# Decode step with a mixer MLP: the last rows of w4 in six small loads behind wq

## The chip, the core and the metric

The kernel runs on one core of one Trainium2 chip. Its time is the device time of one execution in microseconds; shown is the median of several runs. A profile is taken of one execution, and the times inside it count from the start of its span.

The core has a matrix engine (TensorE, PE in the profile), a vector engine (DVE), a scalar engine (ACT), GpSimd (POOL) and a queue engine (SyncE, SP), which issues nearly all transfers here. Transfers run on 16 DMA engines. Each of them works through the pieces (packets) that it was given in the order in which the transfers were issued, and leaves a mark in the trace when its share of a transfer has landed.

## The reference

Two branches start from the layer-normed token xn (1 x 512). The first is an attention over the last 4096 places of the cache, 32 heads of 128. The second is a mixer MLP; with one token all its shifted parts are zero.

```
xn = layernorm(x)
q  = xn @ wq                                  # 512 x 4096
s  = softmax(q . k_window / sqrt(128)) . v_window, heads joined, @ wo
x1 = xn + shifted(gelu(layernorm(xn) @ w1)) @ w2   # the shifted part is 0
h2 = gelu(layernorm(x1) @ w3) @ w4            # w3: 512 x 1376, w4: 1376 x 512
out = x + s * silu(x1 + h2)
```

Weights and caches are bf16. The windows of keys and values are 32 MB each, wq and wo 4 MB each, w2, w3 and w4 3.3 MB together.

## The kernel before

Heads are worked on in eight groups of four (G = 4). A group's keys are one tile of 4 MB (128 partitions of 32 KB), and so are its values. In step s (the loop at the end of the kernel) group s gets its scores and group s - 2 its weighted values (LAG = 2). Scores are split between engines: DVE multiplies and reduces 64 to 80 of the 128 columns (`k_vector`, L329 and L331), and TensorE turns the rest (L345), ACT copies them (L347) and TensorE multiplies (L353). The softmax and the sums over values follow one and two steps behind.

Before the loop TensorE works through the MLP and then q, in the order of the program: the first layer's products with w3 into `a_ps` (L236), the gelu on ACT (L239 to L241), the sum `hr_ps` over w2 (L250) and w4 (L255), its spreading over partitions (L156), then the 128 products of `qT_ps` with wq (L271), and the spreading of q over partitions (L283), which the first product of DVE (L329) needs.

w4 has 1376 rows: 1024 in eight chunks of 128 (`w4_sb`), 32 in a ninth, and 320 extra rows in eight chunks of 40 (NE = 5, 8 x NE = 40). These last are `w4_few`, a tile of 64 partitions with eight rows of w4 (8 KB) on each partition that is used. L97 loads them in two transfers of 20 partitions, onto partitions 0 to 19 and 32 to 51, in an order of rows [...]. The other partitions are zeroed on POOL (L94), which the first of the two waits for. Since the rows then lie in another order than the gelu's results, a small matrix `few`, made from the identity on DVE (L184 to L186), reorders those in a matmul (L243), and a cast (L246) brings them back to bf16.

All large loads go through one function (L79) on the queue of SP, in the order of the program: w2, w3, w4, w4's ninth chunk, w4_few, wq, then the keys of group 0 in two halves, the keys of groups 1 and 2, then values and keys in turn, with wo between them. Transfers take eight semaphores in turn, so each waits for the landing of the one that had its semaphore before. Key tiles have three buffers and value tiles two, the latter in the memory that the weights leave (`wts`).

Of the kernel before, what the change touches and what calls it, by code (L numbers as in the profile page):

```python
# [8 lines left out]
P = 128  # L9
BF16 = mybir.dt.bfloat16  # L10
FP32 = mybir.dt.float32
# [10 lines left out]
NE = 5  # L22
# [7 lines left out]
def kernel(  # L30
# [14 lines left out]
    nc = tc.nc  # L45

    Bb, Sq, D = A_x.shape
# [18 lines left out]
    const = ctx.enter_context(tc.tile_pool(name="const", bufs=1))  # L66
    small = ctx.enter_context(tc.tile_pool(name="small", bufs=1))
    ps_misc = ctx.enter_context(tc.tile_pool(name="ps_misc", bufs=1, space=PSUM))
# [7 lines left out]
    wts = wts_guard.__enter__()  # L76

    def load(dst, src):
        return tc.keep_in_program_order(nc.sync.dma_start(out=dst, in_=src))  # L79
# [10 lines left out]
    w4_sb = wts.tile([P, 9, D], BF16, name="w4_sb")  # L90
    load(w4_sb[:, 0:8, :], B_w4[0:8 * P, :].rearrange("(p c) n -> p c n", p=P))
    load(w4_sb[0:32, 8, :], B_w4[F - 32:F, :])
    w4_few = wts.tile([64, 8, D], BF16, name="w4_few")
    nc.gpsimd.memset(w4_few[:], 0.0)  # L94
    for c in range(2):
        f0 = 8 * P + 32 * NE * c
        load(w4_few[32 * c:32 * c + 4 * NE],  # L97
             B_w4[f0:f0 + 32 * NE, :].rearrange("(b a t) n -> a b (t n)", b=4, a=NE))
    wq_sb = wts.tile([P, KC, HD], BF16, name="wq_sb")

    load(wq_sb[:].rearrange("p c n -> p (c n)"), A_wq.rearrange("(a b c) n -> b a (c n)", a=4, c=KC))

    def load_kv(pool, cache, g, cuts=(0, CP)):
        t = pool.tile([P, CP, Dh], BF16, tag="kv", name="kv")
        src = cache[0, G * g:G * g + G, W0:, :].rearrange("a (b c) d -> b a (c d)", b=PB)
        dst = t[:].rearrange("p c d -> p (c d)")
        for c0, c1 in zip(cuts, cuts[1:]):
            load(dst[:, c0 * Dh:c1 * Dh], src[:, :, c0 * Dh:c1 * Dh])
        return t

    ident_bf = const.tile([P, P], BF16, name="ident_bf")
# [68 lines left out]
        return xc, negmean, rstd  # L180


    few = const.tile([P, 2, 32], BF16, name="few")
    nc.vector.memset(few[:], 0.0)  # L184
    for c in range(2):
        nc.vector.tensor_copy(  # L186
            out=few[:, c, 0:4 * NE].rearrange("p (a b) -> p a b", b=4),
            in_=ident_bf[:, 4 * NE * c:4 * NE * (c + 1)].rearrange("p (b a) -> p a b", b=4))

    x_f = small.tile([P, KC], FP32, name="x_f")  # L190
    nc.vector.tensor_copy(out=x_f[:], in_=x_bf[:])
    xc, negmean, rstd = ln_stats(x_f[:], "x")
# [18 lines left out]
    for j in range(KC):  # L211
        for c in range(KC):
            nc.tensor.matmul(hs_ps[:, j:j + 1], lhsT=w2_sb[:, c, j::4],
                             rhs=shifted_bf[:, c:c + 1], start=(c == 0), stop=(c == KC - 1))
# [19 lines left out]
    for j, m in enumerate(chunks):  # L234
        for c in range(KC):
            nc.tensor.matmul(a_ps[0:m, j:j + 1], lhsT=w3_cols(c, j), rhs=z3_bf[:, c:c + 1],  # L236
                             start=(c == 0), stop=(c == KC - 1))
    a_bf = small.tile([P, 17], BF16, name="a_bf")
    nc.scalar.activation(out=a_bf[:, 0:8], in_=a_ps[:, 0:8], func=ACT.Gelu_apprx_tanh)  # L239
    nc.scalar.activation(out=a_bf[0:32, 8:9], in_=a_ps[0:32, 8:9], func=ACT.Gelu_apprx_tanh)  # L240
    nc.scalar.activation(out=a_bf[0:8 * NE, 9:17], in_=a_ps[0:8 * NE, 9:17], func=ACT.Gelu_apprx_tanh)  # L241
    af_ps = ps_misc.tile([64, 8], FP32, tag="misc", name="af_ps")
    nc.tensor.matmul(af_ps[:], lhsT=few[0:8 * NE].rearrange("p a b -> p (a b)"), rhs=a_bf[0:8 * NE, 9:17],  # L243
                     start=True, stop=True)
    af_bf = small.tile([64, 8], BF16, name="af_bf")
    nc.vector.tensor_copy(out=af_bf[:], in_=af_ps[:])  # L246

    hr_ps = ps_misc.tile([1, D], FP32, tag="misc", name="hr_ps")
    for c in range(KC):
        nc.tensor.matmul(hr_ps[:], lhsT=shifted_bf[:, c:c + 1], rhs=w2_sb[:, c, :], start=(c == 0),  # L250
                         stop=False)
    for i, m in enumerate(chunks):
        act = a_bf[0:m, i:i + 1] if i < 9 else af_bf[:, i - 9:i - 8]
        w = w4_sb[0:m, i, :] if i < 9 else w4_few[:, i - 9, :]
        nc.tensor.matmul(hr_ps[:], lhsT=act, rhs=w, start=False,  # L255
                         stop=(i == len(chunks) - 1))
    hr = wts.tile([1, D], FP32, name="hr")
    nc.vector.tensor_copy(out=hr[:], in_=hr_ps[:])  # L258
# [10 lines left out]
    for h in range(H):  # L269
        for c in range(KC):  # L270
            nc.tensor.matmul(qT_ps[:, h:h + 1], lhsT=wq_sb[:, c, h * Dh:(h + 1) * Dh],  # L271
                             rhs=xq_bf[:, c:c + 1], start=(c == 0), stop=(c == KC - 1))
# [7 lines left out]
    for i in range(0, H // G, 4):  # L280
        qb_ps = ps_tr.tile([P, 4, Dh], FP32, tag="pt", name="qb_ps")
        for k in range(4):
            nc.tensor.matmul(qb_ps[:, k, :], lhsT=sel[:, i + k, :, :].rearrange("k b a -> k (b a)"),  # L283
                             rhs=q_rows[:], start=True, stop=True)
# [355 lines left out]
```

## Time and profile before

| | |
|---|---|
| median of 8 runs | 195.96 us (194.87 to 196.84) |
| profiled execution | 195.74 us |
| its span | 193.9 us |
| busy: PE, DVE, ACT, POOL | 134.3, 145.6, 90.1, 5.9 us |
| moved by DMA | 79.08 MB, mean 408 GB/s |
| granted TensorE clock, mean | 0.708 |

The page gives busy times of each engine, the span in 40 slices, the transfers by queue, and the chain of work that ended last. Busy shares are averages over stages with different limits, so the prediction reads single instructions and what released them. A row of a view of instructions has its start and its length in us, the engine, the line, the operation, what it writes and reads, and in brackets how long the engine had been idle and what ended that. SP's rows are issues: how long the queue engine took to hand a transfer over, and not how long the transfer took.

### The profile page before, as it was taken

What the parts mean: (1) busy time and instruction counts of PE and PEld (TensorE: products, weight loads), DVE (VectorE), ACT (ScalarE), POOL (GpSimd) and SP (SyncE); (2) the same over time, 40 slices, a digit from 0 to 9 for tenths busy, and PEclk for the clock granted to TensorE, in tenths of its full rate; (3) what the DMA queues carried; (4) which work ended last, traced back from release to release, by engine and by line L of the source; (5) the groups of instructions that cost most, each with busy time, mean ns of one, the idle gap of its engine ahead of it and who ended that gap; (6) DMA issues with size and microseconds to landing.
All of it is one profiled execution on the core that took longest, in us unless ns stands there. A gap on an engine that the chain in (4) does not pass through costs nothing.

```text
span 193.9 us, 3919 instructions
## 1 busy us (share of the span) xinstructions
PE 134.3 (69%) x1696; PEld 96.1 (50%) x1696; DVE 145.6 (75%) x168; ACT 90.1 (46%) x197; POOL 5.9 (3%) x12
## 2 busy tenths in 40 slices
PE   0548978868646169159858882983696979886892
PEld 0447257657545144057438442941593358635281
DVE  1580013999999999998999999997999996952011
ACT  2002003887868165318856850681368156863100
POOL 8210000000000000000000000000000000000000
PEclk9999995797955555856797566558558885566675
DMA  5999999999999999999999999999999999999980
GB/s 197 416 442 433 426 429 436 427 429 433 433 431 433 433 429 433 433 433 433 429 433 429 433 433 395 466 433 433 429 426 427 422 433 389 466 405 372 399 304 0
DMA packets 4722, 79.08 MB, mean 408 GB/s; under 512 B 666, under 2 KB 1210, under 8 KB 1722
## 3 DMA queue, kind: packets, MB, share of 16 engines
q1 hardware_dynamic: 4554, 78.84, 95.7%
q8 instruction: 13, 0.21, 0.4%
q10 hardware_dynamic: 152, 0.00, 0.0%
q14 instruction: 3, 0.02, 0.0%
HBM read 78.84 MB, written 0.00 MB: 407 GB/s over the span
## 4 chain that ended last, share of the span: by engine, by line
DVE 51%; PE 27%; DMA 14%; issue 4%; ACT 2%; POOL 0%; POOLq 0%; ACTq 0%; SPq 0%
DVE S L331 29%; DVE prod L329 16%; DMA kv<-in_A_k_cache_dram 12%; PE oT L447 4%; PE pt L345 4%; PE ov L431 3%; PE hr_ps L255 3%; PE a_ps L236 2%; DMA x_bf<-in_A_x_dram 2%; PE oT L440 2%; PE qT_ps L271 2%; ACT kt L347 2%; PE y_ps L156 1%; PE sT L353 1%; PE hr_ps L250 1%
## 5 line engine op out<-in xcount | busy, mean ns | idle before, releaser
L331 DVE TENSOR_REDUCE S<-prod 128x20 f32<-128x2560 bf16 (+2 forms) x32 | 82.2, 2570 | 1.1
L347 ACT COPY kt<-pt 128x1024 bf16<-128x1024 bf16 (+1 forms) x56 | 54.6, 1007 | 17.4 <-PE pt L345 16.7
L345 PE MATMUL pt<-ident_bf,kv 128*128 128x128 bf16 x444 | 47.5, 278 | 3.9 <-DMA kv<-in_A_k_cache_dram 3.8
L329 DVE TENSOR_TENSOR prod<-kv,q_bc 128x2560 bf16<-128x2560 bf16 (+2 forms) x32 | 43.5, 1361 | 2.6 <-ACT q_bc L285 1.3
L345 PEld LDWEIGHTS <-kv 128*128 128x128 bf16 x444 | 38.7, 128 | 8.2 <-DMA kv<-in_A_k_cache_dram 4.8
L353 PE MATMUL sT<-qT_bf,kt 128*128 128x4 bf16 x444 | 20.7, 168 | 15.0 <-ACT kt L347 14.1
L353 PEld LDWEIGHTS <-kt 128*128 128x128 bf16 x444 | 17.2, 104 | 22.8 <-ACT kt L347 22.6
L431 PE MATMUL ov<-kv,pT 128*16 128x512 bf16 x224 | 23.2, 589 | 0.0
L447 PE MATMUL oT<-fold,ov_sb 128*128 128x4 f32 x56 | 10.8, 316 | 14.5 <-DVE rden L402 13.6
L447 PEld LDWEIGHTS oT<-fold,ov_sb 128*128 128x128 f32 x56 | 10.2, 273 | 15.6 <-DVE rden L402 14.0
L391 ACT ACTIVATE pT<-S,mb 128x128 bf16<-128x128 f32 x32 | 14.0, 584 | 0.3
L431 PEld LDWEIGHTS <-pT 128*16 128x16 bf16 x224 | 6.7, 123 | 14.6 <-issue 14.5
L461 ACT ACTIVATE o<-oT,rden 128x1 bf16<-128x1 f32 x20 | 3.6, 264 | 20.9 <-PE oT L447 20.9
L435 ACT COPY ov_sb<-ov 128x512 f32<-128x512 f32 x7 | 4.1, 585 | 16.4 <-PE ov L431 16.4
L362 ACT ACTIVATE own<-sT,par 128x48 f32<-128x48 f32 (+2 forms) x32 | 7.6, 358 | 3.6 <-PE sT L353 3.6
L457 DVE TENSOR_TENSOR o<-oT,rden 128x4 bf16<-128x4 f32 x3 | 0.5, 162 | 11.0 <-PE oT L447 8.5
L391 ACT ACTIVATION_READ_ACCUMULATOR pT<-S,mb 128x1 f32 x32 | 8.6, 267 | 0.0
L239 ACT ACTIVATE a_bf<-a_ps 128x8 bf16<-128x8 f32 x1 | 0.2, 177 | 14.4 <-PE a_ps L236 14.4
L384 PE MATMUL mb_ps<-md,par_t 5*128 5x4 f32 x16 | 4.2, 331 | 3.7 <-DVE md L379 3.7
L375 PE MATMUL mt_ps<-ident_f,m 128*1 128x128 f32 x8 | 2.8, 347 | 4.4 <-DVE rden L402 4.4
L236 PE MATMUL a_ps<-z_bf,w_sb 128*128 128x1 bf16 (+2 forms) x68 | 4.8, 204 | 1.5 <-DVE z_bf L219 1.5
L258 DVE COPY hr<-hr_ps 1x512 f32<-1x512 f32 x1 | 0.7, 678 | 6.8 <-PE hr_ps L255 6.8
(119 smaller groups left out, 101.6 us busy)
## 6 DMA issues: line engine op xcount, KB each, us to landing
kv<-in_A_k_cache_dram SPq DMA_DIRECT2D x7, 4096.0 KB, 31.7
kv<-in_A_v_cache_dram SPq DMA_DIRECT2D x7, 4096.0 KB, 29.9
wq_sb<-in_A_wq_dram SPq DMA_DIRECT2D x1, 4096.0 KB, 16.5
kv<-in_A_k_cache_dram SPq DMA_DIRECT2D x2, 2048.0 KB, 20.7
wo<-in_A_wo_dram SPq DMA_DIRECT2D x1, 2048.0 KB, 26.6
kv<-in_A_v_cache_dram SPq DMA_DIRECT2D x1, 2048.0 KB, 9.7
w_sb<-in_B_w_dram SPq DMA_DIRECT2D x1, 1376.0 KB
w_sb<-in_B_w_dram SPq DMA_DIRECT2D x1, 1024.0 KB, 9.0
```

What stands on the lines that cost most here:

```text
L236: nc.tensor.matmul(a_ps[0:m, j:j + 1], lhsT=w3_cols(c, j), rhs=z3_bf[:, c:c + 1], start=(c == 0), stop=(c == KC - 1))
L255: nc.tensor.matmul(hr_ps[:], lhsT=act, rhs=w, start=False, stop=(i == len(chunks) - 1))
L329: nc.vector.tensor_tensor(out=prod[:, 0:m, :], in0=kn[:, rows, :], in1=q_bc[:, g:g + 1, :].to_broadcast([P, m, Dh]), op=ALU.mult)
L331: nc.vector.tensor_reduce(out=st[g]["S"][:, rows], in_=prod[:, 0:m, :], axis=AX.X, op=ALU.add)
L345: nc.tensor.transpose(pt[:, c - c0, :], kn[:, c, :], ident_bf[:])
L347: nc.scalar.copy(out=kts[b][:, 0:c1 - c0, :], in_=pt[:, 0:c1 - c0, :])
L353: nc.tensor.matmul(st[g]["sT"][:, c - nd(g), :], lhsT=kt[:, c - c0, :], rhs=qT_bf[:, G * g:G * g + G], start=True, stop=True)
L362: nc.scalar.mul(s["own"][:, 0:m, a], s["sT"][:, 0:m, a], par[:, a:a + 1])
L384: nc.tensor.matmul(mb_ps[:], lhsT=par_t[:].rearrange("k b a -> k (b a)"), rhs=md[:], start=True, stop=True)
L391: nc.scalar.activation(out=s["pT"][:, :, a], in_=s["S"][:], func=ACT.Exp, scale=scale, bias=mb[:, a:a + 1], accum_out=s["sum"][:, a:a + 1])
L431: nc.tensor.matmul(s["ov"][r:r + 4 * G], lhsT=s["pT"][:, c:c + 4, :].rearrange("p i a -> p (i a)"), rhs=v[:, c:c + 4, :], start=False, sto ...
L447: nc.tensor.matmul(s["oT"][:], lhsT=s["ov_sb"][:, j, :], rhs=fold[:, G * j:G * j + G], start=(j == 0), stop=(j == 3))
```

## The change

The extra rows of w4 are loaded behind wq and in their plain order: partition p holds rows 1024 + 8 p to 1024 + 8 p + 7. The tile has 40 partitions, and six transfers of 25, 4, 4, 3, 2 and 2 partitions fill it. The first runs on five DMA engines with five packets each, each other one on as many engines as it has partitions[...]: 10, 10, 8, 7 and 5 packets on engines 0 to 4, where now each of them has 8. The memset of the tile, the matrix `few`, its matmul and the cast behind it go away, and the sum over w4 takes the gelu's results as they are.

```diff
-    w4_few = wts.tile([64, 8, D], BF16, name="w4_few")
-    nc.gpsimd.memset(w4_few[:], 0.0)
-    for c in range(2):
-        f0 = 8 * P + 32 * NE * c
-        load(w4_few[32 * c:32 * c + 4 * NE],
-             B_w4[f0:f0 + 32 * NE, :].rearrange("(b a t) n -> a b (t n)", b=4, a=NE))
+    w4_few = wts.tile([8 * NE, 8, D], BF16, name="w4_few")
     wq_sb = wts.tile([P, KC, HD], BF16, name="wq_sb")
 
     load(wq_sb[:].rearrange("p c n -> p (c n)"), A_wq.rearrange("(a b c) n -> b a (c n)", a=4, c=KC))
+    p0 = 0
+    for n in (25, 4, 4, 3, 2, 2):
+        load(w4_few[p0:p0 + n], B_w4[8 * (P + p0):8 * (P + p0 + n), :].rearrange("(p t) n -> p t n", t=8))
+        p0 += n
...
-    few = const.tile([P, 2, 32], BF16, name="few")
-    nc.vector.memset(few[:], 0.0)
-    for c in range(2):
-        nc.vector.tensor_copy(
-            out=few[:, c, 0:4 * NE].rearrange("p (a b) -> p a b", b=4),
-            in_=ident_bf[:, 4 * NE * c:4 * NE * (c + 1)].rearrange("p (b a) -> p a b", b=4))
...
-    af_ps = ps_misc.tile([64, 8], FP32, tag="misc", name="af_ps")
-    nc.tensor.matmul(af_ps[:], lhsT=few[0:8 * NE].rearrange("p a b -> p (a b)"), rhs=a_bf[0:8 * NE, 9:17],
-                     start=True, stop=True)
-    af_bf = small.tile([64, 8], BF16, name="af_bf")
-    nc.vector.tensor_copy(out=af_bf[:], in_=af_ps[:])
...
-        act = a_bf[0:m, i:i + 1] if i < 9 else af_bf[:, i - 9:i - 8]
         w = w4_sb[0:m, i, :] if i < 9 else w4_few[:, i - 9, :]
-        nc.tensor.matmul(hr_ps[:], lhsT=act, rhs=w, start=False,
+        nc.tensor.matmul(hr_ps[:], lhsT=a_bf[0:m, i:i + 1], rhs=w, start=False,
                          stop=(i == len(chunks) - 1))
```

## The prediction

> **What bounds the kernel now.** I read the page's slices and chain first, then the vector engine's instructions in order of time, then the issues of the sync queue, then TensorE's first 34 us, and last the landing marks that the trace keeps for every transfer: one for each DMA engine that took part.
>
> The page's transfer slices and its chain:
>
> ```profile
> DMA  5999999999999999999999999999999999999980
> ...
> DVE 51%; PE 27%; DMA 14%; issue 4%; ACT 2%; POOL 0%; POOLq 0%; ACTq 0%; SPq 0%
> ```
>
> The transfer engines are full from the first slice to the last but two, and yet the chain is mostly DVE. The two meet in one place, which the vector engine's instructions show:
>
> ```profile
> 133.97 0.29 DVE L369 TENSOR_REDUCE m<-S 128x1 f32<-128x128 f32 x1
> 135.24 1.49 DVE L329 TENSOR_TENSOR prod<-kv,q_bc 128x2560 bf16<-128x2560 bf16 x1 [0.99 <-DMA kv<-in_A_k_cache_dram]
> ```
>
> After the scores of group 5 DVE stands idle 0.99 us for the keys of group 6. The transfer's marks run from 131.86 (first engine) to 135.22 (last): DVE waits for the slowest of 16 engines, which is 3.36 us behind the fastest. Before this point DVE works nearly without a gap from 32.66 on, and each earlier key tile landed ahead of its use (k5: landed 110.91, used 115.60). After it comes a fixed row of compute to the end. So the time is what the slowest engine needs up to k6, plus about 60 us; a later start of DVE is free up to 0.99 us.
>
> Where the spread comes from: wq's marks are ten at 20.05 to 20.41, one at 21.89 and five at 22.45 to 22.65. The five are those that carried w4_few just ahead of wq, 8 packets of 8 KB each: 2.4 us, 0.31 us a packet (the packets are recorded at 309 to 356 ns, most near 310). This lag is still there 110 us later, since the rings are never empty. Two of the five are pushed back further, by 0.98 us before k1 lands and by 0.63 us before the first values land, beside packets of the instruction queue q14 at 35.4 and 57.3.
>
> The third view is the start, sync queue and TensorE:
>
> ```profile
> 4.41 1.73 SPq L79 DMA_DIRECT2D w_few<-in_B_w_dram  x2
> 6.18 0.60 SPq L79 DMA_DIRECT2D wq_sb<-in_A_wq_dram  x1
> 6.83 4.32 SPq L79 DMA_DIRECT2D kv<-in_A_k_cache_dram  x4
> ```
> ```profile
> 18.28 0.16 PE L243 MATMUL af_ps<-a_bf,few 40*64 40x8 bf16 x1 [0.37 <-ACT a_bf L241]
> 18.69 1.86 PE L250 MATMUL hr_ps<-w_sb,shifted_bf 128*1 128x512 bf16 x4 [0.25 <-DVE af_bf L246]
> 20.35 3.26 PE L255 MATMUL hr_ps<-w_sb,a_bf 128*1 128x512 bf16 x9
> 23.54 1.88 PE L255 MATMUL hr_ps<-w_few,af_bf 64*1 64x512 bf16 x8
> ...
> 27.14 3.41 PE L271 MATMUL qT_ps<-xq_bf,wq_sb 128*128 128x1 bf16 x128 [0.41 <-DVE bv L263]
> ```
>
> The reader should see that q (L271) stands behind the MLP's last sum (L255) on TensorE, and that w4_few, in place since 12.93, holds nobody up at 23.54.
>
> **The change part by part.** The sum is made against the profiled execution: 195.74 us, of which the span is 193.9 and 1.84 lie around it. The median is 195.96, 0.22 more.
>
> *Removed.* The memset of w4_few on POOL (3.51 us) held only w4_few's own issue; the rings still had w4 until 10.59. Two copies (0.24 us together) and a memset for `few` on DVE lie in its waits before 12 us. Nothing for both; without that cover 0.3 us on DVE, still inside the 0.99. The matmul at L243 and the cast behind it take 18.28 to 18.69 on the path to q: hr_ps starts 0.41 us earlier, and w4_few is wanted at 23.13.
>
> *Four more DMAs and their waits.* The eight lanes of completion semaphores shift. The later small loads now wait for x, w2, w3, w4 (the last at 10.59); k0's first half waits for w4's tail (10.82), its second half for wq (20.4 to 21.9), k1 and k2 for the first two w4_few loads. Queued behind each on SP are all later key loads. But k0's first half is on the rings by 12 and takes 4.9 us of every engine after wq (20.05 to 24.92 in the marks), and an issue reaches the engines in about 1.3 us (w2: 0.73 to 2.03). So second half and k1 (issued about 22 and 24) come in time: nothing. Without that cover each us of empty ring costs a us at k6.
>
> *Packets.* 25 rows on five engines are 5 each[...]. Engines 0 and 1 carry 2 packets more than now: 2 x 0.31 = +0.63 us. Engine 2 the same, engine 3 -0.31, engine 4 -0.94. If only packet counts mattered, k6 would be late by 0.63 if a pushed-back engine is 0 or 1.
>
> *Where the packets go.* [...] the rows at 310 ns next to wq's 32 KB at 1213 ns show no collision[...]
>
> By packet counts alone w4_few is complete at 20.1 + 3.13 = 23.2, TensorE waits 0.1 us, and k6 moves by +0.4 to +0.63. [...] Ends: nothing and +3.8. [...]
>
> *TensorE behind it.* With w4_few at 26.4 TensorE stands from 23.1 on; its last eight matmuls, h2, q (3.41), the broadcast and DVE's first product queue behind. Within L255 matmuls start 427 ns apart until 22.48 and 215 after. [...] Kept: 26.4 + 7 x 0.215 + 0.38 = 28.3 against 25.42 now, +2.9; dropped: 26.4 + 7 x 0.427 + 0.63 = 30.0, +4.6. Less the 0.99 of idle before k6: +1.9 or +3.6. Both run beside the transfers' +3.8 and don't add.
>
> *Sum.* The later of the two: +3.8[...]. k7 follows, as DVE needs 19.85 us from k6 to k7 and k7 landed at 155.06 for a use at 155.09; the last value tiles shift alike. 195.74 + 3.8 = 199.5, at the median 199.7.
>
> Also: what lies behind `few` and the copy of it moves by 128 to 160 bytes a partition, the value tiles among them. No row here times a tile at another offset; I take nothing.
>
> **Rivals.**
> *[...]packets count.* For it: no colliding row in the trace. TensorE hardly waits; k6 +0.4 to +0.63: 196.2 to 196.6, not slower by what can be told. [...]
> *Half of it.* [...] 197.4.
> *The right engines are spared.* If the two pushed-back engines are 2 and 3[...], the slowest becomes 0 or 1 at 3.1 instead of 3.36: -0.2, 195.7. More than 0.99 could not be gained here anyhow, as DVE's own work then sets k6.
> *The rings run dry* behind the new waits. Against it: the 4.9 us of cover. It would add to the first case, at most 2 us: 201.7.
>
> **How the numbers follow.** [...] 0.62 (with the dry rings' 0.04 in it); half 0.10; counts alone 0.20; spared 0.05; something faster that I don't see 0.03. Within 0.5% (0.98 us) is about what a measurement can't tell from no change. Slower: 0.62 + 0.10 + 0.02 of the third = 0.74; same 0.22; faster 0.04. The likeliest case alone has 198.7 to 200.6. The range 196.1 to 200.9 leaves out 0.14 below (the last two cases and a part of the third) and 0.05 above.
>
> **What would show it.** Right: packets of 8 KB of 0.6 to 1.6 us after wq; w4_few's last mark near 26.4; L255's eight matmuls starting there and L258 after 28; k6's marks spread over 6 to 7 us; DVE's wait before k6 of several us or a first product near 36. Wrong: those packets at 0.31, the last mark at 23.2, and k6 landing within 0.7 of 135.22; or a ring without packets between 20 and 30.

## The result

The changed kernel takes 197.79 us (median of 11 runs, 197.53 to 201.24) where the kernel before takes 195.11 us in the same comparison (median of 32 runs). The ratio is 1.0142, with a 95% interval from 1.0114 to 1.0170: slower by 1.4%. The profiled execution of the changed kernel took 197.55 us with a span of 195.7 us, against 195.74 and 193.9 before: +1.8 us in the two profiles, +2.7 us in the medians (the profiled execution before lies 0.63 above its median, the one after 0.24 below its own). The ratios here are of fast executions alone: one of the changed kernel's eleven (201.24 us) and the profiled one of own_counts6 further on (198.22 us) fell into a slower state and are left out of them.

The page's transfer slices and its chain, after:

```profile
DMA  6999999999999999999999999999999999999960
GB/s 206 447 418 420 296 425 455 420 435 425 429 439 417 442 429 419 442 442 429 425 429 435 432 429 402 452 435 429 439 429 429 420 429 390 467 415 400 394 243 4
...
DVE 48%; PE 22%; DMA 20%; ACT 4%; SPq 2%; issue 2%; ACTq 0%
```

The row of busy transfer engines looks as before: no gap in it. But the row below has one slice of 296 GB/s among slices of mostly 417 to 455, the fifth, from about 19.6 to 24.5 us. The engines are busy there and move a third less. The view by stretches shows it closer (columns: stretch, its length, busy time of PE, its weight loads, DVE, ACT and POOL, granted clock, busy share of the transfer engines, GB/s). Before:

```profile
20.00:22.00 2.00, 2.00 (x6) 0.57 (x5) 0.00 (x0) 0.00 (x0) 0.00 (x0) 1.00 0.88 369
22.00:24.00 2.00, 2.00 (x9) 0.57 (x8) 0.00 (x0) 0.00 (x0) 0.00 (x0) 1.00 1.06 451
24.00:26.00 2.00, 1.42 (x7) 0.47 (x6) 0.54 (x1) 0.00 (x0) 0.00 (x0) 1.00 1.00 426
```

After:

```profile
20.00:22.00 2.00, 2.00 (x6) 0.63 (x5) 0.00 (x0) 0.00 (x0) 0.00 (x0) 1.00 1.24 336
22.00:24.00 2.00, 1.49 (x4) 0.20 (x2) 0.00 (x0) 0.00 (x0) 0.00 (x0) 1.00 0.76 201
24.00:26.00 2.00, 0.60 (x3) 0.27 (x4) 0.00 (x0) 0.00 (x0) 0.00 (x0) 1.00 1.04 434
```

The packet records of that stretch (they carry a size and a time, but no engine) say what is slow. The 8 KB packets of w4_few mostly start at 309 to 325 ns and go up to 600 to 850 ns. The 16 KB packets of the first half of group 0's keys (k0), which other engines move at the same time and which otherwise take 611 to 620 ns, take 0.7 to 1.6 us between 20.9 and 23.6 us, all of them.

The landing marks carry this through. The six loads of w4_few left five, four, four, three, two and two of them, at 21.61 to 23.67, 22.44 to 23.15, 23.15 to 23.82, 24.25 to 24.36, 24.57 to 24.66 and 25.06 to 25.15; the two loads before left five each. A mark has a time but no number of its engine, so engine 0, engine 1 and so on are the author's names here and in what stands above. w4_few's last mark is at 25.15. k0's first half has its marks at 26.16 (first) to 29.97 (last), where before it had 24.92 to 27.53: the fastest engine is 1.24 us later and the slowest 2.44. Group 6's keys land at 133.07 to 137.50, before 131.86 to 135.22: 1.21 later on the fastest engine and 2.28 on the slowest.

The sync queue, TensorE's start and DVE, after:

```profile
2.63 0.64 SPq L79 DMA_DIRECT2D wq_sb<-in_A_wq_dram  x1
3.31 7.46 SPq L79 DMA_DIRECT2D w_few<-in_B_w_dram  x6
10.81 14.06 SPq L79 DMA_DIRECT2D kv<-in_A_k_cache_dram  x4
```
```profile
19.66 3.83 PE L241 MATMUL hr_ps<-w_sb,a_bf 128*1 128x512 bf16 x9
25.40 2.65 PE L241 MATMUL hr_ps<-w_few,a_bf 40*1 40x512 bf16 x8 [1.91 <-DMA w_few<-in_B_w_dram]
30.02 3.55 PE L257 MATMUL qT_ps<-xq_bf,wq_sb 128*128 128x1 bf16 x128 [0.41 <-DVE bv L249]
```
```profile
35.69 1.23 DVE L315 TENSOR_TENSOR prod<-kv,q_bc 128x2048 bf16<-128x2048 bf16 x1 [1.29 <-ACT q_bc L271]
...
137.56 1.48 DVE L315 TENSOR_TENSOR prod<-kv,q_bc 128x2560 bf16<-128x2560 bf16 x1
...
157.64 1.23 DVE L315 TENSOR_TENSOR prod<-kv,q_bc 128x2048 bf16<-128x2048 bf16 x1 [0.26 <-DMA kv<-in_A_k_cache_dram]
```

TensorE now waits 1.91 us for w4_few, q follows later, and DVE's first product starts at 35.69 instead of 32.66 (+3.03). At group 6 DVE no longer shows a wait: it comes 2.32 us later than before (137.56 against 135.24), just after the keys (137.50). At group 7 it does wait 0.26 us for the keys. So there are now two paths of nearly the same length, the late start of DVE (135.24 - 0.99 + 3.03 = 137.28) and the late keys (137.50). Which of them costs the time, and which part of the change makes it, is what the experiments ask.

### The profile page after: what moved, and what is told of

It reads as the page before. It is cut to its first block, busy times and chain, and to the rows that moved or that the text cites. A ratio compares the mean times of both kernels' runs of the same rounds, so it can differ in the third digit from the quotient of the medians.

```text
span 195.7 us, 3918 instructions
## 1 busy us (share of the span) xinstructions
PE 136.7 (70%) x1695; PEld 97.5 (50%) x1695; DVE 144.9 (74%) x164; ACT 90.3 (46%) x197; POOL 2.4 (1%) x11
## 4 chain that ended last, share of the span: by engine, by line
DVE 48%; PE 22%; DMA 20%; ACT 4%; SPq 2%; issue 2%; ACTq 0%
DVE S L317 29%; DVE prod L315 15%; DMA wo_rows<-in_A_wo_dram 8%; DMA w_few<-in_B_w_dram 7%; PE pt L331 5%; DMA w_sb<-in_B_w_dram 5%; PE oT L433 4%; ACT kt L333 3%; PE ov L417 3%; SPq L79 2%; PE yr_ps L481 2%; PE sT L339 2%; PE qT_ps L257 2%; PE hr_ps L241 1%; DVE S L353 1%
## 5 line engine op out<-in xcount | busy, mean ns | idle before, releaser
L331 PE MATMUL pt<-ident_bf,kv 128*128 128x128 bf16 x444 | 48.7, 283 | 2.6 <-DMA kv<-in_A_k_cache_dram 2.6
L331 PEld LDWEIGHTS <-kv 128*128 128x128 bf16 x444 | 39.7, 131 | 7.4 <-DMA kv<-in_A_k_cache_dram 3.5
L417 PE MATMUL ov<-kv,pT 128*16 128x512 bf16 x224 | 22.4, 572 | 0.3 <-DMA kv<-in_A_v_cache_dram 0.3
L228 PEld LDWEIGHTS <-w_sb 128*128 128x128 bf16 (+2 forms) x68 | 5.0, 165 | 1.6 <-issue 1.5
## 6 DMA issues: line engine op xcount, KB each, us to landing
kv<-in_A_v_cache_dram SPq DMA_DIRECT2D x7, 4096.0 KB, 23.9
```

What stands on the lines that cost most here:

```text
L331: nc.tensor.transpose(pt[:, c - c0, :], kn[:, c, :], ident_bf[:])
L417: nc.tensor.matmul(s["ov"][r:r + 4 * G], lhsT=s["pT"][:, c:c + 4, :].rearrange("p i a -> p (i a)"), rhs=v[:, c:c + 4, :], start=False, sto ...
```

## The experiments

The theory: the partitions decide. Where the extra rows are written makes the packets of w4_few and those of the keys beside them slow each other, as both were slow at once above; such a stretch is called a collision. The prediction's own sum for it was the author's estimate, on an assumption about which engines slow each other that no trace had shown, so the experiments vary the partitions. The rivals: it is the place behind wq, or the number of packets on each engine, or the late start of q alone. Marks are landing marks in us; "k6" is the keys of group 6. In swap_two and foreign_two w4_few is counted without the spare loads.

| kernel | ratio to before (95%) | w4_few last | k0 first and last | k6 last | DVE's first product |
|---|---|---|---|---|---|
| before | 1 | 12.93 | 24.92, 27.53 | 135.22 | 32.66 |
| after | 1.0142 (1.0114 to 1.0170) | 25.15 | 26.16, 29.97 | 137.50 | 35.69 |
| own_behind | 0.9993 (0.9972 to 1.0014) | 22.53 | 24.87, 27.42 | 135.21 | 33.46 |
| own_counts6 | 0.9983 (0.9963 to 1.0003) | 22.67 | 24.85, 27.57 | 135.15 | 32.58 |
| own_counts | 1.0130 (1.0067 to 1.0194) | 23.06 | 27.86, 28.11 | 136.50 | 32.41 |
| two_writers | 1.0151 (1.0096 to 1.0206) | 25.04 | 27.36, 29.84 | 137.75 | 33.47 |
| six_ahead | 1.0121 (1.0064 to 1.0177) | 14.44 | 27.58, 29.12 | 136.73 | 32.58 |
| after_qfirst | 1.0124 (1.0087 to 1.0162) | 25.12 | 26.42, 29.96 | 137.50 | 35.09 |
| late_own | 1.0292 (1.0257 to 1.0327) | 27.47 | 24.86, 26.54 | 135.26 | 38.30 |
| swap_two | one run, 196.71 us | 22.52 | 24.91, 28.55 | 136.08 | 33.47 |
| foreign_two | one run, 197.10 us | 22.48 | 26.00, 29.70 | 137.30 | 32.66 |
| eight_even | 1.0008 (0.9977 to 1.0038) | 11.94 | 24.70, 26.56 | 135.05 | 32.61 |
| eight_qfirst | 1.0022 (0.9985 to 1.0059) | 11.81 | 24.73, 26.51 | 135.14 | 27.50 |

In late_own k0 goes ahead of w4_few, so its marks stand for less work than in the other rows.

### The place alone: own_behind

The layout and the two loads of the kernel before, put behind wq:

```diff
+    wq_sb = wts.tile([P, KC, HD], BF16, name="wq_sb")
+
+    load(wq_sb[:].rearrange("p c n -> p (c n)"), A_wq.rearrange("(a b c) n -> b a (c n)", a=4, c=KC))
     for c in range(2):
...
-    wq_sb = wts.tile([P, KC, HD], BF16, name="wq_sb")
-
-    load(wq_sb[:].rearrange("p c n -> p (c n)"), A_wq.rearrange("(a b c) n -> b a (c n)", a=4, c=KC))
```

> The kernel before with its two loads of w4_few moved behind wq; same rows, partitions and counts. [...] 8 KB packets stay at 0.31 us, the first half of the first keys lands from 24.9 on, w4_few is complete near 22.6 and TensorE doesn't wait; the same time as before within 0.3%. Place theory (loads of few engines beside the key loads are slow wherever they write): a dip in GB/s near 21 us as in the changed kernel (296 in one slice), first keys from 26 on, 1 to 2% slower.

Measured: 195.16 us against 195.20. w4_few lands at 22.53, the k0 marks are those of before, and DVE starts 0.8 us later, inside its 0.99. The place behind wq costs nothing that can be told (0.9972 to 1.0014).

### The counts alone: own_counts and own_counts6

The counts 10, 10, 8, 7 and 5, behind wq, onto the partitions of the kernel before: 0 to 19 in its first load's order, then every fourth one of 32 to 48, 33 to 45, 34 to 46 and 35 to 43, and at last 0, 4, 1 and 5 of a second tile. The rows lie in another order than the factors, and those in w4_more aren't used in the sum.

```diff
-    for c in range(2):
...
+    w4_more = wts.tile([8, 8, D], BF16, name="w4_more")
+    load(w4_few[0:4 * NE], B_w4[8 * P:8 * P + 32 * NE, :].rearrange("(b a t) n -> a b (t n)", b=4, a=NE))
+    f0 = 8 * P + 32 * NE
+    for t, q, n in ((w4_few, 32, 5), (w4_few, 33, 4), (w4_few, 34, 4), (w4_few, 35, 3), (w4_more, 0, 2), (w4_more, 1, 2)):
+        load(t[q:q + 4 * n - 3:4], B_w4[f0:f0 + 8 * n, :].rearrange("(p t) n -> p t n", t=8))
+        f0 += 8 * n
```

> Behind wq, counts 10, 10, 8, 7, 5 on engines 0 to 4 as in the changed kernel (loads of 20, 5, 4, 4, 3, 2, 2 partitions)[...]. Four partitions' rows stay out of the sum and the others meet other results of the gelu, so its output is another one. [...] packets at 0.31 us, complete near 23.3, key marks of group 0 spread over 3.2 us; keys of group 6 complete 0 to 0.6 us later than before: same within 0.4%. Place or counts theory: 1 to 1.5% slower, as the changed kernel.

Measured: 198.53 us, but not for the reason asked about. It makes seven loads where the change makes six. With eight semaphores in turn, the seventh moves the wait for wq from k0's second half to its first half. The sync queue of own_counts:

```profile
4.41 4.18 SPq L79 DMA_DIRECT2D w_few<-in_B_w_dram  x5
...
20.42 2.80 SPq L79 DMA_DIRECT2D kv<-in_A_k_cache_dram  x4
```

The first key load goes out at 20.42 instead of about 11, the engines that had finished stand still, and k0's first mark is at 27.86, 3 us late. This is the price of dry rings (engines with nothing queued) that the prediction had as a rival. DVE then waits for the keys of group 6 and again for those of group 7:

```profile
157.63 1.23 DVE L331 TENSOR_TENSOR prod<-kv,q_bc 128x2048 bf16<-128x2048 bf16 x1 [1.27 <-DMA kv<-in_A_k_cache_dram]
```

The 8 KB packets themselves all took 309 to 316 ns, ten on one engine too. So I repeated it with six loads: the last of the list goes, the counts of engines 0 and 1 fall from 10 to 9, and two rows of 8 KB are not loaded at all.

```diff
-    w4_more = wts.tile([8, 8, D], BF16, name="w4_more")
+    w4_more = wts.tile([5, 8, D], BF16, name="w4_more")
...
-    for t, q, n in ((w4_few, 32, 5), (w4_few, 33, 4), (w4_few, 34, 4), (w4_few, 35, 3), (w4_more, 0, 2), (w4_more, 1, 2)):
+    for t, q, n in ((w4_few, 32, 5), (w4_few, 33, 4), (w4_few, 34, 4), (w4_few, 35, 3), (w4_more, 0, 2)):
```

> own_counts without the load that made its first keys wait for wq: counts 9, 9, 8, 7, 5 in six loads (20, 5, 4, 4, 3, 2), [...]behind wq. Two rows of 8 KB are not loaded and four partitions' rows are left out of the sum. Collision theory: packets at 0.31 us, last mark of w4_few near 22.8, first key mark at 24.9 as before, keys of group 6 complete at 135.0 to 135.6: same as before within 0.3%. If the counts or the six loads cost the time: 1 to 1.5% slower.

Measured: 195.23 us against 195.60, no difference. Nearly the same counts, the same number of loads, the same place: nothing is lost that can be told (0.9963 to 1.0003) when the rows go onto these partitions, and the packets took 309 to 319 ns.

### Onto partitions 20 to 39: two_writers

Behind wq as in own_behind, and eight packets on each of the five engines as before, but both loads onto partitions 20 to 39. The second load has a tile of its own that the sum doesn't read, so half of the extra rows are left out, and the factors meet other rows.

```diff
+    w4_fewb = wts.tile([64, 8, D], BF16, name="w4_fewb")
+    for c, t in enumerate((w4_few, w4_fewb)):
         f0 = 8 * P + 32 * NE * c
-        load(w4_few[32 * c:32 * c + 4 * NE],
+        load(t[20:20 + 4 * NE],
              B_w4[f0:f0 + 32 * NE, :].rearrange("(b a t) n -> a b (t n)", b=4, a=NE))
```

> As own_behind, 8 packets on each of five engines, but on partitions 20 to 39 of two tiles[...]. The sum then takes half of the rows, and on other partitions than their factors. [...] 1 to 2% slower than before, and slower than own_behind by as much. Place theory: as own_behind.

Measured: 198.42 us. By stretches:

```profile
20.00:22.00 2.00, 2.00 (x6) 0.56 (x5) 0.00 (x0) 0.00 (x0) 0.00 (x0) 1.00 1.05 217
22.00:24.00 2.00, 2.00 (x6) 0.45 (x4) 0.00 (x0) 0.00 (x0) 0.00 (x0) 1.00 0.89 184
24.00:26.00 2.00, 2.00 (x9) 0.56 (x8) 0.00 (x0) 0.00 (x0) 0.00 (x0) 1.00 1.02 377
```

and DVE at group 6:

```profile
137.77 1.49 DVE L330 TENSOR_TENSOR prod<-kv,q_bc 128x2560 bf16<-128x2560 bf16 x1 [2.37 <-DMA kv<-in_A_k_cache_dram]
```

Half the rate for four microseconds and more. All five engines needed about 2.45 us for four packets, 0.61 us each instead of 0.31 (nearly all are recorded at 0.62 to 0.65), where I had expected that of three of them and 0.31 of the other two. And k0's first mark, that of the fastest of all 16 engines, moves by 2.44 us; the spread between first and last stays 2.48. So the loss isn't that of a few engines alone: every engine lost it. I had this only as a possibility, and swap_two and foreign_two, below, ask about it. There was no late q here: DVE started at 33.47, inside its slack.

### The six loads ahead of wq: six_ahead

The six loads of the changed kernel, ahead of wq:

```diff
-    load(wq_sb[:].rearrange("p c n -> p (c n)"), A_wq.rearrange("(a b c) n -> b a (c n)", a=4, c=KC))
     p0 = 0
...
+    load(wq_sb[:].rearrange("p c n -> p (c n)"), A_wq.rearrange("(a b c) n -> b a (c n)", a=4, c=KC))
```

> The changed kernel with its six loads put ahead of wq; same rows, partitions and counts. [...] they collide with each other and with wq instead of the keys: 8 KB packets of 0.5 to 0.9 us, wq's first mark at 21 or later (20.05 before), the keys of group 6 complete near 137; but w4_few is in place long before TensorE wants it, so DVE starts near 32.3: 0.8 to 1.3% slower than before. Place theory: no dip, first mark of wq at 20.1, same as before.

Measured: 197.72 us. w4_few is complete at 14.44, TensorE doesn't wait for it and DVE starts at 32.58, as before. But wq's first mark is at 22.67 where it was at 20.05, on the fastest of the engines, and DVE waits for group 6:

```profile
136.75 1.49 DVE L315 TENSOR_TENSOR prod<-kv,q_bc 128x2560 bf16<-128x2560 bf16 x1 [2.58 <-DMA kv<-in_A_k_cache_dram]
```

The run does not show that the collisions cost this time. With four more loads ahead of it, wq takes its turn on the semaphore of w4's main load, so its issue waits until that has landed (10.39). It goes out at 10.41, before at 6.18. The sync queue and the page's transfer slices of six_ahead:

```profile
2.80 5.34 SPq L79 DMA_DIRECT2D w_few<-in_B_w_dram  x6
10.41 0.64 SPq L79 DMA_DIRECT2D wq_sb<-in_A_wq_dram  x1
```
```profile
DMA  6979999999999999999999999999999999999980
GB/s 209 412 252 430 423 430 430 425 436 426 430 433 431 430 426 430 430 450 436 426 430 433 423 430 399 450 436 430 433 430 430 435 430 388 457 433 403 403 320 16
```

The third slice, from about 9.8 to 14.6 us, has the gap: the engines without w4_few stand still (from 10 to 11.5 us the busy share of all 16 is 0.31), and wq's first packets start at 11.87, before at 9.70. So 2.17 of the 2.62 us are dry rings, as in own_counts. Most of w4_few's packets, 24 of the 35 recorded, ran in that gap, nearly all at 309 ns. The first packets of wq do take up to 2.0 us instead of 1.2 to 1.4, but after the gap of own_counts, without a collision, k0's first packets are slow too (up to 1.4 us instead of 0.61). What six_ahead does show is that late keys cost time without a late q.

### A late q beside the collisions, and a late q alone: after_qfirst and late_own

after_qfirst is the changed kernel with the q products (L257 to L271) ahead of the sum `hr_ps`, so that they don't stand behind w4_few:

```diff
-    hr_ps = ps_misc.tile([1, D], FP32, tag="misc", name="hr_ps")
...
     qT_ps = ps_misc.tile([P, H], FP32, tag="misc", name="qT_ps")
...
+    hr_ps = ps_misc.tile([1, D], FP32, tag="misc", name="hr_ps")
...
```

> The changed kernel with the products of q put ahead of the sum over w4 in the program, so that q no longer waits for w4_few. Collision theory (the time goes into transfers that all 16 engines lose): DVE starts at 30 or earlier, its wait for the keys of group 6 comes back with 3 to 5 us, and these land at 137 to 138 as in the changed kernel; 1.1 to 1.4% slower than before. Late-q theory (the time goes into TensorE's wait for w4_few): back to the time before, within 0.3%.

Measured: 197.75 us, the changed kernel's time. Group 6's keys land at 137.50 as in the changed kernel, and DVE waits for them again:

```profile
137.53 1.49 DVE L315 TENSOR_TENSOR prod<-kv,q_bc 128x2560 bf16<-128x2560 bf16 x1 [0.84 <-DMA kv<-in_A_k_cache_dram]
```

The early start I expected of DVE did not come: `hr` (the copy of `hr_ps`) stands ahead of the first product on DVE, and starts at 33.54 now that the sum runs last, so the product starts at 35.09. It is 0.6 us earlier than in the changed kernel and the wait at group 6 is 0.84: the transfers set this kernel's time.

late_own is the opposite: the partitions of the kernel before, where own_behind lost nothing, but the two loads behind k0's first half.

```diff
+    kn_0 = load_kv(k_pool, A_k_cache, 0, (0, 64))
+    for c in range(2):
+        f0 = 8 * P + 32 * NE * c
+        load(w4_few[32 * c:32 * c + 4 * NE],
+             B_w4[f0:f0 + 32 * NE, :].rearrange("(b a t) n -> a b (t n)", b=4, a=NE))
...
```

> The kernel before [...] w4_few complete only near 27.4. Collision theory: 8 KB packets at 0.31 us, the keys of group 6 land at 135.2 as before; what is left is the late start of DVE (36.5 to 38 against 32.7), of which 1 us is free: up to 1.5 to 2% slower if that start decides alone. A late start as in the changed kernel (35.7) would cost about 2 us, so both paths of the changed kernel would be about as long.

Measured: 201.11 us against 195.84. The keys of group 6 land at 135.26, as before. TensorE and DVE:

```profile
27.51 3.15 PE L257 MATMUL hr_ps<-w_few,af_bf 64*1 64x512 bf16 x8 [3.03 <-DMA w_few<-in_B_w_dram]
```
```profile
38.30 1.23 DVE L331 TENSOR_TENSOR prod<-kv,q_bc 128x2048 bf16<-128x2048 bf16 x1 [1.29 <-ACT q_bc L287]
...
139.81 1.48 DVE L331 TENSOR_TENSOR prod<-kv,q_bc 128x2560 bf16<-128x2560 bf16 x1
```

DVE starts 5.64 us later than before. Less the 0.99 of slack that is 4.65; at group 6 DVE is 4.57 later (139.81 against 135.24), and the medians differ by 5.3. Where the other 0.7 arises behind group 6 I have not followed. So a late start of DVE costs by itself, nearly one for one beyond the slack. In the changed kernel it would cost, as an estimate from this, about 3.03 - 0.99 = 2.0 us if the transfers had lost nothing, and it lies beside their 2.28.

### Who is slowed: swap_two and foreign_two

Both are own_behind (one profiled execution each, so only marks and packets are read) with four more loads of two rows each into a tile that nothing reads. In swap_two they write to partitions 4 to 7 and 32 to 35, which are among those of own_behind's w4_few (0 to 19 and 32 to 51), in foreign_two to partitions 20 to 27, which are not. The other case of swap_two's expectation, 0.6 us a packet and a first mark at 26, is that packets are slow wherever they go onto other partitions than in own_behind's order.

```diff
+    spare = wts.tile([64, 8, D], BF16, name="spare")
+    for i in range(4):
+        load(spare[4 + i:33 + i:28], B_w4[16 * i:16 * i + 16, :].rearrange("(p t) n -> p t n", t=8))
```
```diff
+    spare = wts.tile([64, 8, D], BF16, name="spare")
+    for i in range(4):
+        load(spare[20 + i:25 + i:4], B_w4[16 * i:16 * i + 16, :].rearrange("(p t) n -> p t n", t=8))
```

> own_behind and after it four more loads of two rows (8 KB each) that are read by nobody[...]. Collision theory: 0.31 us a packet, and the first mark of the first keys stays at 24.9. [...] 0.6 us a packet and a first mark at 26.

> As swap_two, [...]. Both theories: about 0.6 us a packet. Collision theory with a hold-up of all engines: the first mark of the first keys moves from 24.9 to about 26.1 [...]. Without the hold-up: [...]the others land from 24.9 on.

Measured, by stretches, swap_two:

```profile
22.00:24.00 2.00, 2.00 (x6) 0.46 (x4) 0.00 (x0) 0.00 (x0) 0.00 (x0) 1.00 1.07 451
```

foreign_two:

```profile
22.00:24.00 2.00, 2.00 (x9) 0.57 (x8) 0.00 (x0) 0.00 (x0) 0.00 (x0) 1.00 1.15 270
```

In both there are eight more packets of 8 KB, from about 22.2 us on. In swap_two they take 309 to 315 ns (six of eight are recorded; last marks of the four loads 22.64, 22.96, 23.27, 23.61) and k0's first mark is at 24.91, where own_behind has 24.87. In foreign_two they take 436 to 638 ns (six recorded; last marks 23.16, 23.83, 24.47, 25.02), all 16 KB packets of k0 that start between 22.3 and 23.9 take 1.0 to 1.28 us, where in swap_two nearly all take 0.61 to 0.64, and k0's first mark is at 26.00. DVE's start is that of before (32.66), so no late q takes part, and it waits 3.07 us for the keys of group 6. The spread from first to last mark is the same in both, 3.63 and 3.70. So the same eight packets cost nothing on partitions 4 to 7 and 32 to 35, and on 20 to 27 all 16 engines lost about 1.1 us, not only a few. The prediction's account, with only some engines slowed, would have had first marks near 24.9 in both. Which engine writes which partitions of k0 at that time the traces do not show. (In swap_two eight packets of k0 near 24.5 took 0.8 to 1.6 us, after the small loads were through; own_counts6 has such a group as well, own_behind has none, and the cause is open.)

### A version without the odd loads: eight_even and eight_qfirst

Can the simpler arithmetic of the change (no `few`, no reordering matmul) be had without the collisions? The 352 last rows of w4 as 32 partitions of 11 rows, four loads of eight partitions, each onto every fourth partition of the 32, ahead of wq (the edit is against the changed kernel):

```diff
...
+    w4_few = wts.tile([32, NT, D], BF16, name="w4_few")
+    few_rows = B_w4[8 * P:F, :].rearrange("(a b t) n -> b a (t n)", b=4, t=NT)
+    for j in range(4):
+        load(w4_few[j:32:4].rearrange("p t n -> p (t n)"), few_rows[j])
...
```

> All 352 rows of w4 past the first 1024 as 32 partitions of 11 rows, in four loads of 8 partitions ahead of wq, so that engines 0 to 7 get four packets of 11 KB each[...], and the gelu's results fit without `few`. Collision theory: no slow packet; key marks of group 6 complete 0.5 to 0.7 us earlier than before (slowest engine 1.7 us of extra rows in place of 2.5). TensorE has 8 more products with w3 and 2 more in the sum, less the matmul of `few`: DVE starts 0.6 us later. 0.2 to 0.4% faster than before. Rival (any load of a few engines is slow): 1% slower.

> As eight_even, with q's products ahead of the sum over w4: DVE starts about 28, so only the transfers decide up to the keys of group 6 (134.6): 0.3 to 0.5% faster than before. If DVE's own work were the limit, the gain over eight_even would be several us.

Measured: 195.88 and 196.06 us against 195.84: no difference in either, and not the 0.2 to 0.5% that I had expected. The keys of group 6 land at 135.05 and 135.14, nearly as before (135.22). eight_qfirst has the q products ahead of the sum as well, and DVE's first product does start 5 us earlier, but the gain is lost at once:

```profile
27.50 1.23 DVE L311 TENSOR_TENSOR prod<-kv,q_bc 128x2048 bf16<-128x2048 bf16 x1 [1.29 <-ACT q_bc L248]
...
34.63 0.68 DVE L258 COPY hr<-hr_ps 1x512 f32<-1x512 f32 x1 [3.59 <-PE hr_ps L255]
35.23 1.20 DVE L311 TENSOR_TENSOR prod<-kv,q_bc 128x2048 bf16<-128x2048 bf16 x1
...
135.16 1.49 DVE L311 TENSOR_TENSOR prod<-kv,q_bc 128x2560 bf16<-128x2560 bf16 x1 [0.46 <-DMA kv<-in_A_k_cache_dram]
```

The copy of `hr` now stands behind the first product on DVE and waits 3.59 us for the sum, so the second product starts at 35.23, before at 36.24, and a further wait of 1.30 us (at 47.29) takes the rest. So this run does not test what an earlier DVE is worth. I found no version that beats the kernel before.

## Why the prediction was right, and where it was not

*The sum and the sign.* The prediction said 199.7 us, in a range from 196.1 to 200.9, and slower; it is 197.79 us. The mechanism held in kind: the partitions decide, and counts (own_counts6) and place (own_behind) do not. The size was off: +3.8 us was said at group 6 in the profile, and 2.28 came. That the range still holds it is in part luck: the loss of the slowest engine itself was said as 3.8 and came as about 1.2, and a loss of 1.24 common to all engines, put at nothing, made up for half of the miss.

*What bounds the kernel.* Right: experiments move the keys and DVE's start apart from each other (two_writers and six_ahead the keys, late_own the start), and each time DVE at group 6 follows the later of the two.

*Removed work, and the additional waits: nothing.* Right. The nine products ahead of w4_few start at 19.66 instead of 20.35, and TensorE then waits for w4_few anyway. The rings didn't run dry: the sync queue had k0's first half out at about 11. own_counts shows what the cover is worth when one more load shifts the waits: after 3 us of empty rings k6 landed 1.28 us later (136.50), not a us for each us, and its profile was 2.5 us longer, and six_ahead lost 2.17 us in that way at wq.

*Where the packets go.* Right in kind, with two wrong terms. The +3.8 and the 26.4 were the author's estimate, on an assumption that no trace had shown and that no run here tests as such. What the runs show is the time by partitions: 309 to 319 ns on 0 to 19 and from 32 on (own_counts6) and 309 to 315 on 4 to 7 and 32 to 35 (swap_two), 436 to 638 on 20 to 27 (foreign_two) and mostly 0.62 to 0.65 us on 20 to 39 (two_writers).
The first wrong term is the time of the engine with ten packets. The prediction had it finish about 6.3 us after wq, with w4_few's last mark at 26.4. The longest packet took 0.85 us, and the last mark was at 25.15. Packet counts alone had given 23.2.
The second is that it put the loss on some engines alone. By k0's first mark all 16 lose 1.24 us. The slowest ones have nothing to spare, so this part goes straight into the end time. The slowest engine's +2.44 at k0 is this 1.24 and 1.20 of its own. If it is one of the two with ten packets (the marks don't say), two more packets make 2 x 0.31 = 0.62 of that, and the other 0.58 is what its slow packets lost beyond the loss of all.

*TensorE behind it.* w4_few came 1.2 us earlier than said, so that TensorE stood only 1.91 us, but the clock did not stay at full: it fell in the middle of the eight matmuls, which took 2.65 us. The stretches after, with the granted clock third from the end:

```profile
25.50:26.00 0.50, 0.50 (x3) 0.16 (x2) 0.00 (x0) 0.00 (x0) 0.00 (x0) 1.00 1.01 426
26.00:26.50 0.50, 0.50 (x3) 0.16 (x2) 0.00 (x0) 0.00 (x0) 0.00 (x0) 0.88 1.00 426
26.50:27.00 0.50, 0.50 (x3) 0.13 (x2) 0.00 (x0) 0.00 (x0) 0.00 (x0) 0.50 1.00 426
```

The copy of hr started at 28.09, near the 28.3 of the case "kept", but by luck: the matmuls began 1.0 us earlier than said and took 0.8 longer. Before, the clock fell as well, at about 29.3 (0.66 in the stretch from 29 to 30, 0.50 in the next) and with no such stand, so these runs do not show that the stand caused the fall; the case "dropped" was an assumption.

*Beside each other.* The prediction had +1.9 or +3.6 for the start and +3.8 for the transfers, not added. Right in form: about 2.0 (by the estimate under late_own) and 2.28 came, and DVE is 2.32 later at group 6. after_qfirst shows that the transfers alone would have been enough.

*Behind group 6.* "About 60 us fixed" held within half a microsecond: from the first product of group 7 to the output's issue it is 36.1 us before and 35.6 after.

*What would show it.* Packets of 0.6 to 1.6 us: for w4_few they were 0.6 to 0.85, and k0's had the rest. The spread of group 6's marks was to be 6 to 7 us and is 4.4, for the reason just given: a part of the loss is common to all engines and makes no spread.

*The rivals.* "Half of it", 197.4 us, came closest in time, but by another cause: it was the likeliest case with less time lost on the same engines, and what came is a loss of all. In foreign_two (0.44 to 0.64 us) and two_writers (0.62 to 0.65) the packets took up to about twice the 0.31, in the changed kernel at most 0.85.

## What to carry to other kernels

For a load that uses only some of the transfer engines, look at the partitions it is written to, and not only at how many packets each engine has. Here forty packets beside the keys cost nothing on partitions 0 to 19 and 32 to 51 (0.9993 of the time before, own_behind) and 1.5% on 20 to 39 (1.0151, two_writers). Eight packets on 20 to 27 were enough to cost every engine 1.1 us (foreign_two), so read the first landing mark of the large transfer beside a small one too. And after adding or removing a load, count again which earlier transfer each later load now waits for.

## What the runs showed that I had not expected

- A small load onto other partitions held up all 16 engines: 1.24 us in the changed kernel, 1.1 in foreign_two for eight packets of 8 KB, 2.44 in two_writers for forty. Over the stretch of the collision the whole core moves about half: 184 to 217 GB/s in two_writers against 414 to 451 in swap_two. Why all engines slow down isn't settled by these runs.
- The order of semaphores cost about as much as the layout: one load more in own_counts, +1.3% (1.0067 to 1.0194). In six_ahead too it left engines standing.
- A dry ring evened the engines out. In own_counts, where the rings ran dry once, k0's marks were within 0.25 us of each other again, before within 2.61.
